# Pooled attention with a SoLU layer: v as 128 consecutive pooled rows per pair of heads, first loads in another order, all orders planned anew

## The chip, the cores and the metric

One core of one Trainium2 chip runs the whole kernel. Times are device microseconds (us). Lower is better. Three runs of the kernel before gave 516.31, 513.35 and 512.03 us; their median, 513.35 us, is the time that the changed kernel is compared with.

## The reference

Eight batches, eight heads, 576 rows of 64 numbers. k and v are pooled over eight rows each, so that every head has 72 pooled rows:

```python
k_p = k.reshape(B, H, 72, 8, D).mean(axis=3)
v_p = v.reshape(B, H, 72, 8, D).mean(axis=3)
scores = q @ k_p^T / sqrt(D)
attn = softmax(scores)
x = (attn @ v_p), heads side by side     # 4608 tokens x 512
h = x @ w_in                             # w_in 512 x 1024, float64
solu = h * softmax(h)
ln = (solu - mean) / sqrt(var + 1e-6) * g_ln
out = ln @ w_out                         # w_out 1024 x 512, float64
```

The weights arrive as float64; everything else is float32.

## The kernel before, in words

The 4608 tokens are 36 tiles of 128. Every float32 operand of a large product is split into a high and a low half in float16, and a product is taken in three passes (high x high, high x low, low x high). Per tile: `q_hi`, `q_lo` split q, a DMA transpose (`q_T`, L805) turns it, TensorE makes `scores` (L842), VectorE and ScalarE make the softmax (`s_max` L852, `s_sub` L855, `s_exp` L862, `e_sum` L866, `e_rec` L872 and L876, `e_mul` L881), ScalarE and GpSimd split it (`e_hi`, `e_lo`), a DMA transpose turns it (`e_T`, L917), TensorE multiplies it by v (`av`, L928), `x_hi` and `x_lo` (L936, L940) split the result, and `mm1` (L957) multiplies it by w_in in three parts of 8 matmuls. `h_max`, `h_nb`, `h_exp`, `z_mul`, `z_cen`, `z_hi`, `z_lo` make the layer (L967 to L1019), `z_T` (L1027) turns it, `mm2` (L1066) multiplies it by w_out in three parts of 8 matmuls, `o_evac` (L1074) scales it out of PSUM, and a store follows.

PSUM holds one buffer of scores, one of `av`, two of `mm1`'s result and one of `mm2`'s result. So `mm1` of a tile waits for `z_mul` of the tile two before it, and `mm2` of a tile waits for `o_evac` of the tile before it.

Before the first tile, the weights are prepared. Each weight is loaded in four quarters of 1 MiB (`w_load`, L563). A quarter of w_in goes through `w_exp` (ScalarE, L574), `w_shift` (VectorE, L578), `w_bnd` (TensorE, L590), `w_tail` (VectorE, L597), `w_sgn` (ScalarE, L615) and `w_mul` (GpSimd, L618). Only when all four quarters have passed `w_bnd` can the largest value be found (`w_rmax`, `w_par`, `w_all`) and the scale be set (`wi_scale`, last instruction L653). After it `w_hi` (L720), `w_res` (L741) and `w_lo` (L757) write the two halves of w_in that `mm1` reads.

k and v of a batch come in three loads each (`load_kv`): parts 0 and 1 of 512 KB, part 2 of 128 KB. k's lines (L336, L340) put 128 consecutive pooled rows of all heads on 128 partitions. v's lines differ: part 0 (L343) puts rows 0 to 63 of the four even heads on partitions 0 to 63, part 1 rows 0 to 63 of the four odd heads on partitions 64 to 127, and part 2 (L348) puts the last 8 rows of every head on 64 partitions. GpSimd adds the eight rows up in three levels (`pool_kv`, L380); for v, the first level of parts 0 and 1 waits for both loads. `a_max`, `a_par`, `a_all`, `a_scale` find a batch's scale. `v_hi` (L507, ScalarE) and `v_lo` (L513, VectorE) write the split v into `vb`, 64 partitions at a time, `v_rep`, `r_hi`, `r_lo` copy the left-over rows, and `r_put` (GpSimd, L543, two instructions of 256 columns) places them, masked by `rmask`.

All DMAs are issued by SyncE's queue (SP) in one order. The order of every operation is written out by hand in `ORDER`: for each operation name a tuple of positions, and all operations are emitted in order of position. An engine takes its own operations in that order and never overtakes. `load_g` (L673) loads g_ln, 1024 single numbers. In the order before, SP's queue begins (k, v parts in brackets, q halves, w_in quarters w0 to w3, w_out quarters A to D):

```
k[0] k[2] w0 k[1] q0 q1 g w1 w2 v[0] v[1] w3 v[2] B A q_T(1) D C ...
```

VectorE's list between the arrival of w1 and the scale of w_in is, before: `w_shift` w1, `w_tail` w1, `q_lo`(1), k's `a_max`, `w_shift` w2, `q_lo`(3), `w_tail` w2, k's `a_all` and `a_scale`, `k_lo`, `w_shift` w3, `s_scale`, `s_max`, `s_sub`, `w_rmax`, `w_tail` w3, `e_sum`, `e_rec`, `e_mul`, `w_all`, v's `a_max`, `wi_scale`.

Of the kernel before, what the change touches and what calls it, by code (L numbers as in the profile page):

```python
# [1446 lines left out]
```

## Time and profile before

| | us |
|---|---|
| median of three runs | 513.35 |
| profiled execution, whole | 516.21 |
| its span, first to last instruction | 514.4 |
| TensorE (PE) busy in the span | 468.7 (91%) |
| VectorE (DVE) | 366.3 (71%) |
| ScalarE (ACT) | 331.5 (64%) |
| GpSimd (POOL) | 327.6 (64%) |

Times in the rows are of the span. PE is the matmul side of TensorE, PEld its weight loads, SPq SyncE's queue. An arrow in brackets behind a row says how long the engine was idle before it and what it then waited for. The profiled execution ran 1.8 us longer than its span and 2.9 us longer than the median of the three runs.

### The profile page before, as it was taken

Reading aid. Unit: us, or ns where it says so; the run is one execution under the profiler, and the core shown is the slowest. Engines: PE = TensorE matmul, PEld = TensorE weight load, DVE = VectorE, ACT = ScalarE, POOL = GpSimd, SP = SyncE. Lnnn points to the kernel's source line nnn. Section 1 sums busy time; section 2 is a strip of 40 time slices with the busy share of each in tenths; the row PEclk is TensorE's granted clock in tenths of the full one; section 3 lists DMA queues with packets and bytes.
Section 4 is the critical chain, followed back from the end, with each engine's and each line's share of the span. In section 5 each row is a group of like instructions: output and inputs, shape, how many; then the busy total and the mean of one; then the engine's idle time right before and its main releaser. Section 6 shows DMA issues by size and latency. Waiting matters only on the chain.

```text
span 514.4 us, 9219 instructions
## 1 busy us (share of the span) xinstructions
PE 468.7 (91%) x3236; PEld 247.9 (48%) x3236; DVE 366.3 (71%) x777; ACT 331.5 (64%) x515; POOL 327.6 (64%) x554
## 2 busy tenths in 40 slices
PE   0227999999999999999999999999999989999996
PEld 0114545554465555555555555554554445454442
DVE  3669998989778775879588888776568678755230
ACT  2529987877766675667486775667647655667541
POOL 5463778887982767567967678656938335645331
PEclk9999999999999999999999999999999999999999
DMA  7998938696997978898999489978599655655433
GB/s 253 257 276 242 247 65 190 121 213 150 209 204 123 198 166 170 141 223 206 198 173 196 99 138 267 177 158 187 134 184 188 125 114 109 123 106 104 89 90 93
DMA packets 189501, 86.26 MB, mean 168 GB/s; under 512 B 165904, under 2 KB 174096, under 8 KB 188944
## 3 DMA queue, kind: packets, MB, share of 16 engines
q1 hardware_dynamic: 189456, 85.69, 79.2%
q8 instruction: 25, 0.41, 0.3%
q14 instruction: 20, 0.16, 0.1%
HBM read 36.70 MB, written 9.44 MB: 90 GB/s over the span
## 4 chain that ended last, share of the span: by engine, by line
PE 74%; DMA 7%; DVE 5%; ACT 5%; issue 3%; POOL 3%; SPq 2%; POOLq 0%; ACTq 0%; DVEq 0%
PE hp L957 33%; PE op L1066 29%; PE xp L928 6%; DMA wir<-in_moe_w_in_dram 4%; PE sc L842 4%; DMA qT<-q 2%; DMA eT<-e 1%; SPq L563 1%; POOL z L1019 1%; PE res_wi L741 1%; DVE u_wi L578 1%; DVE z L999 1%; PE kTp L475 1%; DVE m L967 1%; SPq L673 1%
## 5 line engine op out<-in xcount | busy, mean ns | idle before, releaser
L1066 PE MATMUL op<-wo,zT 128*128 128x512 f16 x864 | 198.1, 379 | 1.8 <-ACT osb L1074 1.7
L957 PE MATMUL hp<-wi,xT 128*128 128x512 f16 x864 | 196.2, 379 | 0.5 <-ACT xT L936 0.5
L957 PEld LDWEIGHTS <-xT 128*128 128x128 f16 x864 | 83.1, 98 | 97.3 <-ACT xT L936 1.0
L1066 PEld LDWEIGHTS <-zT 128*128 128x128 f16 x864 | 82.3, 98 | 93.4 <-issue 2.5
L1019 POOL TENSOR_TENSOR z<-z,z 128x512 f16<-128x512 f32 x71 | 83.0, 1176 | 59.7 <-ACT z L1013 59.5
L967 DVE TENSOR_REDUCE m<-hp 128x1 f32<-128x1024 f32 x36 | 43.9, 1219 | 30.9 <-PE hp L957 30.7
L906 POOL TENSOR_TENSOR e<-e,e 128x512 f16<-128x512 f32 x36 | 42.3, 1175 | 31.5 <-ACT e L897 31.5
L380 POOL TENSOR_TENSOR vr<-vr 128x512 f32<-128x512 f32 (+3 forms) x48 | 41.6, 875 | 19.3 <-DMA vr<-in_v_dram 18.9
L999 DVE SCALAR_TENSOR_TENSOR z<-hp,rs,z 128x1024 f32<-128x1024 f32 x36 | 46.1, 1280 | 10.8 <-ACT z L978 9.8
L1008 ACT ACTIVATE z<-z,sz 128x1024 f32<-128x1024 f32 x36 | 41.2, 1144 | 17.8 <-DVE z L999 17.7
L978 ACT ACTIVATE z<-hp,nb,Hb 128x1024 f32<-128x1024 f32 x32 | 38.4, 1199 | 19.4 <-DVE nb L970 15.9
L380 POOL TENSOR_TENSOR kr<-kr 128x512 f32<-128x512 f32 (+3 forms) x48 | 42.2, 886 | 12.5 <-DMA kr<-in_k_dram 11.6
L1074 ACT ACTIVATE osb<-op,f 128x512 f32<-128x512 f32 x36 | 24.5, 680 | 24.6 <-issue 16.1
L852 DVE TENSOR_REDUCE mx<-sc 128x8 f32<-128x576 f32 x36 | 27.1, 752 | 17.2 <-PE sc L842 17.2
L928 PE MATMUL xp<-eT,vb 128*128 128x128 f16 (+1 forms) x640 | 38.2, 214 | 0.8 <-DMA eT<-e 0.8
L1013 ACT ACTIVATE z<-z 128x1024 f16<-128x1024 f32 x36 | 37.8, 1051 | 1.2 <-DMA zT<-z 0.6
L928 PEld LDWEIGHTS <-vb 128*128 128x128 f16 x640 | 34.8, 98 | 7.2 <-DMA eT<-e 1.3
L1032 ACT ACTIVATE junk<-z 128x1024 f16<-128x1024 f32 x36 | 37.7, 1047 | 0.1
L897 ACT ACTIVATE e<-e 128x512 f16<-128x512 f32 x36 | 22.4, 623 | 20.3 <-DVE e L881 14.0
L866 DVE TENSOR_REDUCE sc<-sc 128x8 f32<-128x576 f32 x36 | 27.4, 761 | 9.7 <-ACT sc L862 9.6
L936 ACT ACTIVATE xT<-xp 128x512 f16<-128x512 f32 x36 | 21.3, 591 | 19.9 <-PE xp L928 19.7
L940 DVE SCALAR_TENSOR_TENSOR xT<-xp,xT 128x512 f16<-128x512 f32 x36 | 24.5, 682 | 10.9 <-ACT xT L936 10.9
(226 smaller groups left out, 626.3 us busy)
## 6 DMA issues: line engine op xcount, KB each, us to landing
kr<-in_k_dram SPq DMA_DIRECT2D x16, 512.0 KB, 4.6
qr<-in_q_dram SPq DMA_DIRECT2D x16, 512.0 KB, 5.2
vr<-in_v_dram SPq DMA_DIRECT2D x16, 512.0 KB, 9.7
out_dram<-osb SPq DMA_DIRECT2D x32, 256.0 KB, 3.3
wor<-in_moe_w_out_dram SPq DMA_DIRECT2D x4, 1024.0 KB, 8.4
wo<-in_moe_w_in_dram SPq DMA_DIRECT2D x2, 1024.0 KB
wir<-in_moe_w_in_dram SPq DMA_DIRECT2D x2, 1024.0 KB, 12.1
zT<-z SPq DMA_TRANSPOSE x72, 3.3
```

Source lines behind the costliest of these rows:

```text
L380: nc.gpsimd.tensor_tensor(out=dst, in0=src[:, :, :n], in1=src[:, :, n : 2 * n], op=ALU.add)
L906: nc.gpsimd.tensor_tensor(out=e_main(i, 1), in0=e_src(i)[:, :, :64], in1=e_main(i, 0), op=ALU.subtract)
L928: nc.tensor.matmul(xp[:, c, lo:hi], lhsT=vb[b % 2][:, vt, c].rearrange("p j d -> p (j d)"), rhs=eT[:, n, lo:hi], start=(j == 0), stop=(j = ...
L957: nc.tensor.matmul(hp[:, f], lhsT=xT[:, xt, c], rhs=wi[:, wt, c, f * 512 : (f + 1) * 512], start=(c == 0 and xt == 0 and wt == 0), stop=(c ...
L967: nc.vector.tensor_reduce(out=small(i, "m"), in_=tl[i]["hp"], axis=AX.XY, op=ALU.max)
L978: nc.scalar.activation(z, t["hp"], AF.Exp, bias=t["nb"], scale=hsc(i, 0), accum_out=small(i, "se"))
L999: nc.vector.scalar_tensor_tensor(out=t["z"], in0=t["hp"], scalar=t["rs"], in1=t["z"], op0=ALU.mult, op1=ALU.mult, accum_out=small(i, "sz"),)
L1008: nc.scalar.activation(t["zf"], t["zf"], AF.Identity, bias=t["sz"], scale=-float(DFF))
L1013: nc.scalar.activation(t["z16"][:, 0], t["zf"], AF.Copy)
L1019: eng.tensor_tensor(out=t["z16"][:, 1, fs], in0=t["zf"][:, fs], in1=t["z16"][:, 0, fs], op=ALU.subtract)
L1032: nc.scalar.activation(junk, t["zf"], AF.Square, scale=DFF**-0.5, accum_out=small(i, "V"))
L1066: nc.tensor.matmul(op_, lhsT=zT[:, zt, c], rhs=wo[:, wt, c], start=(c == 0 and zt == 0 and wt == 0), stop=(c == CO - 1 and zt == 1),)
```

## The change

Pooled rows are now counted per pair of heads: a pair has 144 consecutive pooled rows. The first 128 of them lie on 128 partitions, one column block per pair, and the last 16 (all of the odd head) are the left-over rows. Parts 0 and 1 of a v load are two pairs each, 128 partitions by 4 KB; part 2 is the 16 rows of the four pairs, on 64 partitions as before. On the 128 partitions, rows 0 to 71 belong to the even head and rows 72 to 127 to the odd head, so `v_hi` and `v_lo` write all 128 partitions of a head's columns with a scale that is zero outside its rows. A new VectorE operation, `v_msk`, multiplies the batch's scale by a fixed mask of two columns; `v_hi` and `v_lo` wait for it. `r_put` places the left-over rows for the odd heads alone, two instructions of 128 columns. The softmax side (`e_main`, `e_rest`, `e_src`) is cut the same way: four runs of 128 and four of 16 in place of eight of 64 and eight of 8. `v`'s first pooling level of a part waits for that part alone.

The planner's list of first loads is `"01kq2v3gABCD"` in place of `"0kq12v3gABCD"`, and `ORDER` is written anew. SP's queue now begins:

```
k[0] g w0 k[1] q0 k[2] q1 w1 v[0] w2 w3 v[2] v[1] A B q_T(1) C D ...
```

VectorE's list between the arrival of w1 and the scale of w_in is now: `w_shift` w1, `q_lo`(0), `w_tail` w1, `q_lo`(3), k's first `a_scale`, `w_shift` w2, `q_lo`(1), `w_tail` w2, `w_shift` w3, two `a_scale`, `k_lo`, `w_rmax`, `s_max`, `s_sub`, `s_scale`, `e_sum`, `e_rec`, `e_mul`, `w_tail` w3, `w_all`, `wi_scale`, and then v's `a_max`. ScalarE's list there is: `w_exp` w1, `q_hi`(0), `q_hi`(3), `w_sgn` w1, `w_exp` w2, `q_hi`(1), `w_exp` w3, `w_sgn` w2, `k_hi`, `q_Tc`, `w_exp` A, `s_exp`, `w_sgn` B, `w_exp` B, `e_hi`, `w_sgn` w3, `w_dg`, `w_hi`. At the end of the list, TensorE's parts stand as `mm1`(34) part 2, `mm2`(33) parts 1 and 2, `mm2`(32), `mm2`(35), `mm2`(34); before, `mm2`(33) stood ahead of `mm1`(34) part 2.

```diff
 ORDER = {
...
-    "load_g": (6,),
...
-    "load_q": (4, 5, 116, 132, 377, 415, 618, 707, 906, 955, 1171, 1217, 1379, 1425, 1656, 1755),
...
-    "w_load": (2, 7, 8, 20, 30, 28, 57, 55),
...
+    "load_g": (4,),
+    "load_kv": (0, 10, 16, 46, 66, 64, 158, 170, 163, 230, 237, 232, 282, 321, 316, 330, 407,
...
+    "load_q": (12, 24, 152, 154, 426, 438, 640, 703, 901, 933, 1159, 1210, 1410, 1427, 1665, 1762),
...
+    "v_msk": (116, 346, 587, 840, 1100, 1254, 1510, 1861),
...
+    "w_load": (5, 34, 48, 54, 78, 87, 120, 121),
...
+    vmask = const.tile([P, 2], F32, name="vmask")
...
+    for j, cs in enumerate((slice(0, SP), slice(SP, P))):
+        nc.vector.tensor_reduce(out=vmask[:, j : j + 1], in_=ident[:, cs], axis=AX.X, op=ALU.max)
...
+        rows = v[b].rearrange("h (r j) d -> (h r) (j d)", j=POOL).rearrange(
+            "(c r) x -> r c x", c=CI
+        )
         if part < 2:
-            eng.dma_start(
-                t[64 * part : 64 * part + 64, :CI],
-                v[b].rearrange("(c e) (r j) d -> e r c (j d)", e=2, j=POOL)[part, :64],
-            )
-        else:
-            eng.dma_start(
-                t[:64, CI], v[b, :, SA:].rearrange("h (r j) d -> h r (j d)", j=POOL)
-            )
+            eng.dma_start(t[:, c0:c1], rows[:P, c0:c1])
+        else:
+            eng.dma_start(t[:64, CI], rows[P:])
...
+    def v_msk(b):
+        st = grp["v", b]
+        st["sm"] = sm.tile([P, 2], F32, tag="smv", name=f"smv{b}")
+        nc.vector.tensor_scalar(
+            out=st["sm"], in0=vmask, scalar1=st["s"], scalar2=None, op0=ALU.mult
+        )
+
     def v_hi(b, e):
-        r_ = slice(64 * e, 64 * e + 64)
         nc.scalar.activation(
-            vb[b % 2][r_, 0, :, e], vp[b % 2][r_, :CI], AF.Copy, scale=grp["v", b]["s"][r_]
+            vb[b % 2][:, 0, :, e], vp[b % 2][:, :CI], AF.Copy,
+            scale=grp["v", b]["sm"][:, e : e + 1],
         )
...
-                out=vb[b % 2][:, 2, 2 * j : 2 * j + 2].rearrange("p c e d -> p (c e) d"),
-                in0=bat[b]["vr16"][:, j].unsqueeze(1).to_broadcast([P, 4, D]),
-                in1=rmask.unsqueeze(2).to_broadcast([P, 4, D]), op=ALU.mult,
+                out=vb[b % 2][:, 2, 2 * j : 2 * j + 2, 1],
+                in0=bat[b]["vr16"][:, j].unsqueeze(1).to_broadcast([P, 2, D]),
+                in1=rmask.unsqueeze(2).to_broadcast([P, 2, D]), op=ALU.mult,
...
-        return e16[i % 2][:, t * SA : t * SA + SA].rearrange("p (h r) -> p h r", h=H)
+        return e16[i % 2][:, t * SA : t * SA + SA].rearrange("p (c r) -> p c r", c=CI)
...
-            if nm == "v" and part < 2:
-                rk = [("rp", "vr", b, e) for e in range(2)]
...
-    for n, c in enumerate("0kq12v3gABCD"):
+    for n, c in enumerate("01kq2v3gABCD"):
```

## Rows read from the trace of the kernel before

**Rows 1.** Busy time of each engine in stretches of the span, all engines in one line: the stretch and its length in us, then busy us and instructions of PE, PEld, DVE, ACT and POOL, the granted clock, the mean busy share of the DMA engines and GB/s.

```profile
0.00:43.00 43.00, 7.35 (x67) 5.39 (x68) 24.99 (x47) 17.05 (x21) 23.81 (x33) 1.00 0.98 277
43.00:61.00 18.00, 17.84 (x123) 10.33 (x124) 17.45 (x36) 17.80 (x24) 8.56 (x8) 1.00 0.87 213
61.00:80.00 19.00, 17.91 (x115) 9.31 (x112) 16.34 (x39) 16.55 (x27) 14.91 (x22) 1.00 0.49 101
80.00:360.00 280.00, 279.87 (x1980) 148.78 (x1980) 220.92 (x479) 191.85 (x308) 203.27 (x349) 1.00 0.88 178
360.00:480.00 120.00, 117.11 (x822) 61.22 (x821) 78.79 (x164) 76.04 (x121) 68.00 (x124) 1.00 0.69 132
480.00:514.00 34.00, 28.60 (x140) 12.89 (x137) 7.83 (x16) 12.20 (x17) 9.09 (x22) 1.00 0.36 85
```

**Rows 2.** The timeline of ScalarE and VectorE at the arrival of w_in's quarters: start, duration, instruction, and the idle time ahead of it. The first two are `w_exp` of quarter 1 and of quarter 3, the third is `w_shift` of quarter 3.

```profile
17.49 1.13 ACT L574 ACTIVATE u_wi<-wo 128x1024 f32<-128x1024 f32 x1 [0.40 <-DMA wo<-in_moe_w_in_dram]
...
32.26 1.12 ACT L574 ACTIVATE u_wi<-wir 128x1024 f32<-128x1024 f32 x1 [3.22 <-DMA wir<-in_moe_w_in_dram]
...
33.41 3.90 DVE L578 TENSOR_SCALAR u_wi<-u_wi 128x1024 int32<-128x1024 int32 x1 [3.52 <-ACT u_wi L574]
```

**Rows 3.** The timeline from the scale of w_in to the first tile's `mm1`: the last instructions of `wi_scale`, then `x_lo` of tile 0 and the first matmuls of `mm1`.

```profile
43.41 0.26 DVE L653 TENSOR_SCALAR pw<-pwi 128x1 f32<-128x1 f32 x3
...
59.55 0.68 DVE L940 SCALAR_TENSOR_TENSOR xT<-xp,xT 128x512 f16<-128x512 f32 x1
...
60.97 5.34 PE L957 MATMUL hp<-wi,xT 128*128 128x512 f16 x24
```

**Rows 4.** The same table of stretches as rows 1, for three stretches of the first 35 us; the last column is what the DMA engines moved, in GB/s.

```profile
9.00:17.00 8.00, 1.14 (x10) 0.79 (x10) 5.73 (x9) 2.99 (x4) 5.79 (x5) 1.00 1.07 362
19.00:27.00 8.00, 1.34 (x11) 0.95 (x12) 5.30 (x9) 5.31 (x7) 2.50 (x1) 1.00 1.07 169
29.00:35.00 6.00, 1.33 (x24) 1.22 (x23) 2.41 (x2) 1.15 (x2) 5.01 (x5) 1.00 1.20 361
```

**Rows 5.** SP's queue in the timeline: when it issued a load and how long the issue took it: w0, g, w1, and both large parts of v in one row.

```profile
1.95 0.58 SPq L563 DMA_DIRECT2D wo<-in_moe_w_in_dram  x1
...
4.19 3.34 SPq L673 DMA_DIRECT2D g_sb<-in_moe_g_ln_dram  x1
7.57 3.68 SPq L563 DMA_DIRECT2D wo<-in_moe_w_in_dram  x1
...
11.77 1.50 SPq L343 DMA_DIRECT2D vr<-in_v_dram  x2
```

**Rows 6.** The page's list of DMA issues: count, KB each, and the median us from issue to landing.

```profile
kr<-in_k_dram SPq DMA_DIRECT2D x16, 512.0 KB, 4.6
...
vr<-in_v_dram SPq DMA_DIRECT2D x16, 512.0 KB, 9.7
```

**Rows 7.** The timeline of the steps that stand ahead of the scale of w_in: `w_sgn` of quarter 2, `k_hi`, `k_lo`, `scores`, `s_max`, `s_sub`, `s_exp`, `w_tail` of quarter 3, `e_sum`, `e_mul`, `w_all`, and `a_max` of v.

```profile
25.29 1.14 ACT L615 ACTIVATE sg_wi<-wir 128x1024 f16<-128x1024 f32 x1
28.29 0.74 ACT L483 ACTIVATE kT<-kTp,sk 128x576 f16<-128x576 f32 x1 [1.50 <-PE kTp L475]
29.07 0.82 DVE L487 SCALAR_TENSOR_TENSOR kT<-kTp,sk,kT 128x576 f16<-128x576 f32 x1 [1.27 <-ACT kT L483]
...
29.94 1.12 PE L842 MATMUL sc<-kT,qT 128*128 128x72 f16 x16 [1.68 <-DVE kT L487]
...
38.13 0.77 DVE L855 TENSOR_TENSOR sc<-sc,mx 128x576 f32<-128x576 f32 x1
38.99 0.71 ACT L862 ACTIVATE sc<-sc,ct('b', 0)_291 128x576 f32<-128x576 f32 x1 [5.61 <-DVE sc L855]
39.14 1.22 DVE L597 SCALAR_TENSOR_TENSOR wir<-wir,u_wi 128x1024 int32<-128x1024 int32 x1
...
41.51 0.76 DVE L881 TENSOR_TENSOR e<-sc,r 128x576 f32<-128x576 f32 x1
42.18 0.28 DVE L630 TENSOR_REDUCE gm_wi<-g_wi 128x1 f32<-128x128 f32 x1
42.38 0.48 DVE L391 TENSOR_REDUCE amx_v<-vp 128x1 f32<-128x320 f32 x1
```

**Rows 8.** Groups of instructions by line and shape over the whole span (count, busy us, mean ns of one): `r_put` and `v_hi`; then ScalarE's copy of k on 128 partitions.

```profile
L543 POOL TENSOR_TENSOR vb<-vr,rmask 128x256 f16<-128x256 f16 x16 | 9.8, 637 | 3.2 <-DVE vr L536 2.5 <-ACT q L793 0.7
L507 ACT ACTIVATE vb<-vp,sv 64x256 f16<-64x256 f32 x16 | 8.0, 501 | 3.3 <-DVE sv L464 3.2
...
L468 ACT ACTIVATE kp<-kp 128x320 f32<-128x320 f32 x8 | 3.7, 463 | 0.8 <-POOL kp L380 0.8
```

**Rows 9.** What TensorE waited for after 60 us, summed: us in total, times, longest.

```profile
PE op L1066 <- ACT osb L1074: 1.7, 2, 0.9
PE sc L842 <- DMA qT<-q: 1.6, 1, 1.6
...
PE xp L928 <- DMA eT<-e: 0.8, 1, 0.8
```

**Rows 10.** Groups of instructions from the page: `h_max`, `z_mul` and `h_exp`, with the mean ns of one behind the busy time.

```profile
L967 DVE TENSOR_REDUCE m<-hp 128x1 f32<-128x1024 f32 x36 | 43.9, 1219 | 30.9 <-PE hp L957 30.7
...
L999 DVE SCALAR_TENSOR_TENSOR z<-hp,rs,z 128x1024 f32<-128x1024 f32 x36 | 46.1, 1280 | 10.8 <-ACT z L978 9.8
...
L978 ACT ACTIVATE z<-hp,nb,Hb 128x1024 f32<-128x1024 f32 x32 | 38.4, 1199 | 19.4 <-DVE nb L970 15.9
```

More of the change, by code (lines that the diff above doesn't have):

```diff
@@ L153 @@
-    "v_hi": (133, 125, 363, 349, 643, 578, 879, 837, 1170, 1174, 1285, 1297, 1500, 1507, 1833,
-        1826),
-    "v_lo": (151, 147, 371, 376, 655, 665, 894, 892, 1176, 1183, 1289, 1299, 1509, 1513, 1842,
-        1838),
-    "v_rep": (119, 342, 582, 832, 1161, 1280, 1493, 1837),
-    "w_all.wi": (98,),
-    "w_all.wo": (192,),
-    "w_bnd.wi": (22, 45, 75, 80),
-    "w_bnd.wo": (139, 165, 167, 170),
-    "w_dg.wi": (120,),
-    "w_dg.wo": (227, 205),
-    "w_exp.wi": (13, 38, 48, 71),
-    "w_exp.wo": (90, 103, 129, 140),
@@ new lines @@
+    "e_mul": (86, 151, 197, 258, 345, 390, 417, 484, 526, 615, 680, 656, 808, 841, 866, 911, 970,
+        1042, 1105, 1163, 1212, 1276, 1333, 1370, 1477, 1417, 1552, 1642, 1603, 1695, 1750, 1818,
+        1871, 1903, 1986, 1952),
+    "e_rec": (84, 85, 140, 141, 187, 193, 255, 256, 339, 341, 388, 389, 413, 415, 461, 472, 524,
[4 rows of a table added]
+    "e_sum": (83, 136, 186, 249, 334, 387, 412, 459, 523, 610, 676, 646, 796, 819, 863, 906, 966,
+        1026, 1102, 1131, 1197, 1256, 1330, 1357, 1463, 1404, 1526, 1624, 1596, 1690, 1729, 1810,
+        1852, 1891, 1983, 1946),
@@ new lines @@
+    "g_all": (27,),
+    "g_max": (14,),
+    "g_par": (15,),
+    "h_bat": (133, 400, 580, 896, 1178, 1265, 1660, 1867),
+    "h_exp": (215, 296, 350, 398, 452, 513, 554, 706, 649, 746, 772, 912, 928, 949, 1007, 1048,
+        1114, 1216, 1239, 1304, 1363, 1429, 1485, 1547, 1572, 1629, 1698, 1792, 1752, 1835, 1905,
+        1926, 1987, 2018, 2061, 2046),
+    "h_max": (209, 272, 318, 362, 447, 493, 536, 704, 647, 734, 768, 875, 922, 946, 1004, 1021,
+        1112, 1202, 1233, 1295, 1355, 1378, 1476, 1528, 1555, 1612, 1686, 1765, 1723, 1831, 1873,
+        1912, 1977, 2001, 2058, 2038),
@@ new lines @@
+    "h_mix": (402, 903, 1346, 1886),
+    "h_nb": (210, 273, 319, 382, 448, 504, 537, 705, 648, 735, 769, 878, 923, 947, 1005, 1022,
+        1113, 1203, 1236, 1296, 1359, 1395, 1479, 1540, 1556, 1613, 1687, 1766, 1730, 1832, 1875,
+        1913, 1979, 2002, 2059, 2039),
+    "k_T": (58, 280, 571, 695, 1050, 1300, 1437, 1761),
+    "k_dup": (33, 278, 501, 681, 963, 1171, 1408, 1634),
+    "k_hi": (61, 299, 572, 740, 1062, 1301, 1440, 1780),
+    "k_lo": (62, 300, 586, 741, 1063, 1302, 1441, 1786),
@@ new lines @@
+    "r_hi": (137, 356, 591, 850, 1176, 1289, 1518, 1856),
+    "r_lo": (139, 360, 594, 859, 1180, 1291, 1522, 1857),
+    "r_put": (159, 361, 641, 861, 1181, 1293, 1681, 1869),
+    "s_exp": (82, 134, 185, 246, 333, 385, 399, 458, 518, 609, 672, 645, 784, 814, 862, 905, 964,
+        1025, 1101, 1126, 1196, 1255, 1329, 1356, 1461, 1403, 1521, 1623, 1595, 1674, 1728, 1804,
+        1851, 1890, 1975, 1943),
+    "s_max": (74, 105, 169, 212, 311, 365, 396, 446, 503, 589, 670, 624, 766, 812, 845, 877, 953,
+        1009, 1076, 1124, 1174, 1235, 1327, 1350, 1459, 1394, 1506, 1620, 1569, 1671, 1708, 1802,
+        1843, 1884, 1958, 1938),
@@ new lines @@
+    "v_hi": (130, 129, 367, 354, 593, 592, 849, 883, 1127, 1141, 1285, 1263, 1520, 1519, 1862,
+        1863),
+    "v_lo": (149, 148, 375, 376, 607, 596, 880, 893, 1133, 1169, 1299, 1274, 1565, 1563, 1874,
+        1870),
+    "v_msk": (116, 346, 587, 840, 1100, 1254, 1510, 1861),
+    "v_rep": (118, 355, 590, 843, 1175, 1288, 1517, 1846),
+    "w_all.wi": (95,),
+    "w_all.wo": (194,),
+    "w_bnd.wi": (9, 37, 69, 70),
+    "w_bnd.wo": (142, 143, 165, 166),
+    "w_dg.wi": (97,),
+    "w_dg.wo": (228, 202),
@@ new lines @@
+    "w_exp.wi": (6, 35, 49, 55),
+    "w_exp.wo": (79, 89, 122, 127),
+    "w_hi.wi": (145, 108, 126, 175),
+    "w_hi.wo": (205, 201, 303, 309),
+    "w_lo.wi": (176, 135, 174, 191),
+    "w_lo.wo": (252, 240),
+    "w_load": (5, 34, 48, 54, 78, 87, 120, 121),
+    "w_lod.wo": (304, 347),
+    "w_mul.wi": (23, 63, 76, 107),
+    "w_mul.wo": (161, 132, 224, 295),
+    "w_par.wi": (93,),
+    "w_par.wo": (192,),
+    "w_res.wi": (146, 109, 144, 189),
+    "w_res.wo": (229, 220),
+    "w_rmax.wi": (71,),
@@ new lines @@
+    "w_rmax.wo": (180,),
+    "w_sgn.wi": (22, 44, 57, 92),
+    "w_sgn.wo": (160, 88, 196, 294),
+    "w_shift.wi": (7, 36, 50, 56),
+    "w_shift.wo": (110, 111, 150, 147),
+    "w_tail.wi": (8, 41, 53, 94),
+    "w_tail.wo": (131, 128, 162, 204),
+    "wi_scale": (96,),
+    "wo_scale": (200,),
+    "x_hi": (179, 219, 269, 308, 378, 450, 495, 627, 603, 685, 742, 767, 868, 917, 940, 989,
+        1019, 1152, 1204, 1270, 1309, 1336, 1407, 1462, 1537, 1571, 1647, 1724, 1683, 1779, 1816,
+        1883, 1950, 1962, 2041, 2005),
```

245 lines of the change are left out of this document (94 added, 151 removed), and 96 rows, old and new, of the table ORDER.

## The prediction

> **What bounds the kernel now.** I read the table of stretches first [rows 1]. From 80 to 360 us TensorE is busy for 279.87 of 280 us, and from 360 to 480 for 117.11 of 120. No engine can make that part shorter, since the change takes no matmul away. What is left is the head and the end: before 43 us TensorE is busy for 7.35 us, so 35.65 are empty, and 43 to 80 and 480 to 514 hold 1.25 and 5.40 more. A gain of some size can only come out of the 35.65.
>
> Next, what the head waits for. ScalarE idles until each quarter of w_in lands: quarter 1 at 17.49, quarter 3 only at 32.26, after 3.22 us with nothing to do [rows 2]. The scale of w_in needs all four quarters, and it is done at 43.41 + 0.26 = 43.67; the first `mm1` starts at 60.97 [rows 3]. The head is therefore a chain: last quarter landed, 11.41 us to the scale, 17.30 us to `mm1`.
>
> Why does quarter 3 land so late? The rates of the transfers say it [rows 4]: 362 GB/s from 9 to 17 us, 361 from 29 to 35, but 169 from 19 to 27. In that stretch the two large parts of v are under way, issued at 11.77 behind w2 and ahead of w3 [rows 5]. Over the whole run a v load of 512 KB takes 9.7 us to land and a k load of the same size 4.6 [rows 6]. The v loads fill 64 partitions, the k loads 128.
>
> **The change, part by part.** *First loads.* Up to w1 both orders carry the same bytes (k, q, w0, w1: 4.125 MiB), so I keep 17.49 as w1's landing and correct it below for g. Before, w2, v[0], v[1] and w3 (3 MiB) came behind it; now it is v[0], w2 and w3 (2.5 MiB = 2.62 MB), and v no longer on half of the partitions. At 361 GB/s that takes 7.26 us: w3 lands at 24.75. The other end, with v as slow as now: 0.524 MB at 169 GB/s and 2.10 MB at 361 are 8.9 us, 26.4. I take the first, since k's parts already have the shape that v's now get.
>
> g moves from behind q1 to the second place, ahead of w0. Its issue held SP's queue for 3.34 us [rows 5]. In front of w0 it could move w0's issue from 1.95 to about 4.6, 2.65 us; but k[0] is being moved meanwhile, and before the change SP was held from 4.19 to 11.25 by g and w1 in a row, ahead of w1, which no longer stands behind g. Bounds 0 and 2.65; I take 0.5, near the lower end for that reason. So w3 at 25.25, 7.0 us earlier. The queue's other moves (v[2], v[1], A, B and the first q transpose come right behind) are each earlier than now, as the bytes ahead are no more.
>
> *From w3 to the scale.* With w3 this early, the k side is no longer done first: VectorE's new list puts `k_lo` and the softmax of tile 0 behind `w_shift` w3, and `w_tail` w3 and the scale behind that softmax. Link by link: `w_exp` 1.12 [rows 2], then `w_sgn` w2 1.14, `k_hi` 0.74, `k_lo` 0.82, `scores` 1.12, `s_max` about 0.75, `s_sub` 0.77, `s_exp` 0.71, `e_sum` about 0.75 (both like `e_mul`), `e_rec` about 0.4, `e_mul` 0.76, `w_tail` 1.22, `w_all` 0.28 [rows 7], and 0.9 for the scale: 11.5, with some 0.05 at each of ten hand-overs (`k_hi` to `k_lo`, 0.04, [rows 7]) and 0.2 for `q_Tc` 12.2. The same stretch was 11.41, so 0.8 of the 7.0 is given back: scale at 37.5, 6.2 earlier.
>
> *From the scale to `mm1`.* From 43.67 to the start of `x_lo` at 59.55 VectorE works without a pause to speak of [rows 1, 3]. Its list there is the old one plus v's `a_max` (0.48, [rows 7]) and `v_msk` (0.26 for three such small instructions, [rows 3]; 0.15 with its hand-over). 0.6 more is given back: `mm1` starts 5.6 us earlier, at 55.4. From there TensorE is full, as now.
>
> *`v_hi`, `v_lo`.* 128 partitions in place of 64 with the same columns. ScalarE's copy of 320 columns on 128 partitions takes 463 ns, `v_hi` with 256 on 64 takes 501 [rows 8]: partitions cost nothing. *`v_msk`* stands ahead of both once a batch; from the second batch on TensorE's full list covers it. If that cover went, 8 x 0.15 = 1.2 us. *`r_put`* halves its columns, 0.3 us less of GpSimd each of 16 times [rows 8], hidden, as GpSimd idles a third of the span. *The softmax side* has the same elements in longer runs; nothing. *Masks and memsets* fall before 4 us, when everything waits for loads; nothing.
>
> *Steady part.* The v loads of batches 1 to 7 also land faster, and the waits of TensorE for transposes, 1.6 and 0.8 [rows 9], may shrink. Bounds 0 and 2.4; I take 0.8 gained. *End.* TensorE now runs `mm2`(33) straight into `mm2`(32), 35 and 34: three hand-overs of its one PSUM buffer instead of two, each like the 0.9 in rows 9: 0.9 lost.
>
> **Sum.** 7.0 - 0.8 - 0.6 + 0.8 - 0.9 = 5.5 us. Against the profiled execution: span 514.4 to 508.9, whole 516.21 to 510.7. That execution ran 2.9 us over the median of 513.35; the median becomes 507.8.
>
> **The rivals.**
>
> *A, the forecast: 507.8.* Its own range 505.5 to 510, from g (0 to 2.65) and the steady part. 56%.
>
> *B, VectorE gives more back: 511.* `w_shift` w3 took 3.90 us here though ScalarE had long delivered, [rows 2], in a stretch in which GpSimd was busy for 5.01 of 6 us [rows 4]. Were the head's chain hit by one such stretch more, 3.2 us of the 5.5 are gone. For it: GpSimd's new list has pooling and `w_mul` all along. Against: `w_tail` w3 now comes when the pooling of v should be over. 15%.
>
> *C, v gets no faster, only the order counts: 510.* w3 then lands at 26.4 + 0.5, 5.4 earlier; less 0.8, 0.6 and 0.9, and with nothing gained in the steady part, 3.1: 510.2. Against it: k's 4.6 us beside v's 9.7. 9%. [...]
>
> *D, more: 504.8.* g costs nothing (0.5), and all of the waits for transposes go (1.6 more) with the end's third hand-over hidden (0.9): 8.5. 11%.
>
> *E, slower: 519.* The new list starts a tile's `mm1` sooner behind that of two tiles before: at its closest (tiles 14 and 16) one tile's `mm1` and one `av` and `scores` lie between, about 6.6 us, where the closest before was 8.4. In that time `h_max`, `h_exp` and `z_mul` must run, 3.7 us of work [rows 10], and VectorE has other work queued between them. If the new plan is this tight everywhere, TensorE stalls. It decides when the 36 tiles lose over 10.6 us together, 0.3 each, enough to turn the 5.5 into 5.1 lost; at 0.3 to 0.35 each it is 518.6 to 520.4. For it: TensorE has no room. Against: the old list, nearly as tight, loses 0.13 in 280 us [rows 1]. 9%.
>
> **How the numbers follow.** A measurement of this kernel can tell about 1% from no change, 5.1 us; the bound is 508.2. Of A somewhat more than half lies under it (0.33), and D (0.11), with a little of B and C: 0.47 faster. E is 0.09 slower. The rest, 0.44, is within 1%. The predicted time is A's 507.8. The range goes from 504.5 to 512: it takes in B, C and nearly all of A and D and leaves out E and D's lower end.
>
> **What would show it.** Right: v loads land in about 5 us; the rate stays over 330 GB/s until w3; `w_exp` of quarter 3 starts at 24.5 to 27; the scale ends near 37.5 and `mm1` starts near 55.4; TensorE is as full from there as now. Wrong at the first step, if `w_exp` of quarter 3 starts after 28; at the second, if it is early but the scale is after 40; at the third, if `mm1` is early but TensorE's empty time after 61 us grows by more than 2.

## The result, and the profile after

The changed kernel takes 520.43 us, the median of four runs (518.95 to 522.54). The kernel before took 514.75, the median of four runs on the same chip: the three of 513.35 and one more of 516.15. The ratio is 1.0118, with a 95% interval from 1.0081 to 1.0155: slower by about 1.2%, where 507.8, a gain, was forecast, and outside the range of 504.5 to 512. The profiled execution took 521.71 us, with a span of 520.0 against 514.4 before.

The table of stretches of the changed kernel, with the columns of [rows 1]. The last stretch runs 2 us past the end of the span; up to 520 us its clock is 1.00.

```profile
0.00:43.00 43.00, 11.11 (x89) 7.88 (x90) 30.06 (x58) 22.33 (x27) 26.71 (x35) 1.00 1.01 327
43.00:61.00 18.00, 16.99 (x127) 8.59 (x127) 17.59 (x37) 14.98 (x20) 13.58 (x11) 1.00 0.29 71
61.00:80.00 19.00, 16.28 (x96) 8.19 (x93) 15.06 (x30) 15.73 (x28) 15.03 (x22) 0.91 0.61 130
...
80.00:360.00 280.00, 273.80 (x1941) 144.82 (x1941) 227.28 (x476) 185.98 (x300) 196.01 (x338) 1.00 0.81 172
360.00:480.00 120.00, 120.00 (x832) 62.75 (x830) 81.21 (x173) 75.62 (x121) 65.85 (x120) 1.00 0.68 139
480.00:522.00 42.00, 33.15 (x164) 15.07 (x161) 8.36 (x18) 16.12 (x22) 14.42 (x31) 0.98 0.38 88
```

Set against [rows 1], the empty time of TensorE reads as follows. Before 43 us it fell from 35.65 to 31.89, 3.8 gained. From 43 to 80 us it grew from 1.25 to 3.73, and from 80 to 360 from 0.13 to 6.20: 8.6 lost. From 360 to 480 all of the 2.89 went, and the end, up to the end of the span, grew from 5.8 to 6.9. That makes 2.9 us more of empty time, and the busy time grew by 2.65 (471.32 against 468.67), together the 5.6 of the spans. One cell says why the engine was busy for longer with the same products: the granted clock, 0.91 between 61 and 80 us. It accounts for 1.7 of the 2.65; the rows do not explain the other 0.9.

What TensorE waited for after 60 us (us in total, times, longest), to be held against [rows 9]:

```profile
PE op L1076 <- ACT osb L1084: 3.4, 4, 0.9
PE res_wo L751 <- DVE z L1009: 2.7, 1, 2.7
PE sc L852 <- DVE e L891: 2.5, 3, 1.4
```

The waits for transposes of q are gone. In their place stand waits for VectorE, which [rows 9] do not have, and the hand-overs of the output's PSUM buffer have doubled in all: at the end there are three (2.5 us) for two (1.7), and the fourth lies between 80 and 160 us.

The head, in the timeline: `w_shift` of quarter 2, `w_exp` of quarter 3, `w_tail` of quarter 2, `w_shift` of quarter 3, `k_hi`, the last instructions of the scale, and the first product. They answer to [rows 2, 3].

```profile
22.48 2.54 DVE L588 TENSOR_SCALAR u_wi<-u_wi 128x1024 int32<-128x1024 int32 x1
...
23.98 1.15 ACT L584 ACTIVATE u_wi<-wir 128x1024 f32<-128x1024 f32 x1 [1.20 <-DMA wir<-in_moe_w_in_dram]
...
26.09 2.28 DVE L607 SCALAR_TENSOR_TENSOR wir<-wir,u_wi 128x1024 int32<-128x1024 int32 x1
...
28.29 1.21 DVE L588 TENSOR_SCALAR u_wi<-u_wi 128x1024 int32<-128x1024 int32 x1
...
29.85 0.74 ACT L486 ACTIVATE kT<-kTp,sk 128x576 f16<-128x576 f32 x1 [3.70 <-DVE sk L467]
...
39.27 0.26 DVE L663 TENSOR_SCALAR pw<-pwi 128x1 f32<-128x1 f32 x3
...
56.00 1.89 PE L967 MATMUL hp<-wi,xT 128*128 128x512 f16 x8
```

The transfers did what was forecast. In the page's list of DMA issues v now lands like k, in 4.7 us where [rows 6] had 9.7:

```profile
vr<-in_v_dram SPq DMA_DIRECT2D x16, 512.0 KB, 4.7
```

**The costliest place.** The longest single wait, in the timeline: GpSimd's `e_lo` and VectorE's `w_tail` of w_out's last quarter, then `h_max` and `z_mul` of the first tile, then TensorE's `w_res`.

```profile
62.09 1.41 POOL L916 TENSOR_TENSOR e<-e,e 128x512 f16<-128x512 f32 x1 [2.76 <-ACT e L907]
62.40 2.18 DVE L607 SCALAR_TENSOR_TENSOR wor<-wor,u_wo 128x1024 int32<-128x1024 int32 x1
...
64.51 1.21 DVE L977 TENSOR_REDUCE m<-hp 128x1 f32<-128x1024 f32 x1
...
67.46 1.28 DVE L1009 SCALAR_TENSOR_TENSOR z<-hp,rs,z 128x1024 f32<-128x1024 f32 x1 [0.19 <-ACT z L988]
...
69.01 1.69 PE L751 MATMUL res_wo<-wor,dg_wo 128*128 128x512 f32 x2 [2.72 <-DVE z L1009]
```

`w_res` wants the PSUM buffer that holds the first tile's products until `z_mul` has read them. `z_mul` stands behind `h_max`, `h_max` in VectorE's list behind a `w_tail` that took 2.18 us beside GpSimd (1.21 in the kernel before). TensorE stands for 2.72 us. What follows shows in TensorE's own table of single microseconds (busy us, granted clock, DMA share, GB/s):

```profile
68.00:69.00 1.00, 0.00 (x0) 1.00 0.77 223
69.00:70.00 1.00, 0.99 (x2) 0.70 0.71 272
70.00:71.00 1.00, 1.00 (x3) 0.50 0.00 0
71.00:72.00 1.00, 1.00 (x3) 0.50 0.00 0
72.00:73.00 1.00, 1.00 (x3) 0.59 0.00 0
73.00:74.00 1.00, 1.00 (x6) 1.00 0.00 0
```

The engine comes back at a granted clock of 0.50 instead of 1.00 and stays there for some 3.4 us. One minus the clock, summed over these rows, is another 1.71 us lost, without a single empty slot. A table of busy shares alone hides it. In the kernel before the same place had a wait of 1.1 us and a clock of 1.00 throughout. Its `w_tail` of w_out's last quarter, and the `w_res` that waited:

```profile
65.50 1.21 DVE L597 SCALAR_TENSOR_TENSOR wor<-wor,u_wo 128x1024 int32<-128x1024 int32 x1
...
71.05 1.14 PE L741 MATMUL res_wo<-wor,dg_wo 128*128 128x512 f32 x2 [1.09 <-ACT xT L936]
```

### The profile page after: what moved, and what is told of

Same layout as the page of the kernel before. It is cut to its first block, busy times and chain, and to the rows that moved or that the text cites. A ratio compares the mean times of both kernels' runs of the same rounds, so it can differ in the third digit from the quotient of the medians.

```text
span 520.0 us, 9226 instructions
## 1 busy us (share of the span) xinstructions
PE 471.3 (91%) x3236; PEld 247.3 (48%) x3236; DVE 379.6 (73%) x787; ACT 330.8 (64%) x515; POOL 331.6 (64%) x554
## 4 chain that ended last, share of the span: by engine, by line
PE 64%; DVE 22%; ACT 5%; issue 4%; DMA 3%; SPq 1%; POOL 1%; ACTq 0%; DVEq 0%; POOLq 0%
PE op L1076 28%; PE hp L967 26%; PE xp L938 4%; DVE q L807 3%; PE sc L852 3%; DMA wo<-in_moe_w_in_dram 2%; DVE z L1009 2%; DVE m L977 2%; DVE sc L876 2%; DVE e L891 1%; DVE wor L607 1%; DVE sc L865 1%; DVE mx L862 1%; DMA zT<-z 1%; ACT z L988 1%
## 5 line engine op out<-in xcount | busy, mean ns | idle before, releaser
L916 POOL TENSOR_TENSOR e<-e,e 128x512 f16<-128x512 f32 x36 | 43.4, 1204 | 57.0 <-ACT e L907 57.0
L383 POOL TENSOR_TENSOR kr<-kr 128x512 f32<-128x512 f32 (+3 forms) x48 | 44.3, 933 | 13.9 <-DMA kr<-in_k_dram 13.4
L383 POOL TENSOR_TENSOR vr<-vr 128x512 f32<-128x512 f32 (+3 forms) x48 | 43.4, 913 | 9.1 <-DMA vr<-in_v_dram 5.4
L852 PE MATMUL sc<-kT,qT 128*128 128x72 f16 (+1 forms) x640 | 27.2, 201 | 9.5 <-DVE e L891 6.6
L852 PEld LDWEIGHTS <-qT 128*128 128x128 f16 (+1 forms) x640 | 24.7, 104 | 17.3 <-issue 11.7
```

The lines of the kernel that those rows point to most:

```text
L383: nc.gpsimd.tensor_tensor(out=dst, in0=src[:, :, :n], in1=src[:, :, n : 2 * n], op=ALU.add)
L852: nc.tensor.matmul(o, lhsT=t["qT"][:, h, lo:hi], rhs=kT[:, x, h * SP : (h + 1) * SP], start=(x == 0), stop=(x == 1),)
L916: nc.gpsimd.tensor_tensor(out=e_main(i, 1), in0=e_src(i)[:, :, :P], in1=e_main(i, 0), op=ALU.subtract)
```

## The experiments

Theory 1: the new order puts VectorE's instructions with two inputs in SBUF (`q_lo`, with a mean of 0.87 us before and 1.10 in the changed kernel), and fast small ones (`v_msk`, with a median of 0.23 us and 0.83 at the longest), beside GpSimd's work; each is held up, VectorE works in order, and TensorE stops. Theory 2: the new order's own hand-overs of PSUM. Theory 3: the new layout costs it. All edits are against the changed kernel, but for the one of the order alone, and each ratio is to the kernel before, run on the same chip. The runs were made on more than one chip, so where two of them are set against each other, their ratios say more than their times.

**The layout alone.** The order table is that of the kernel before, with the mask behind v's third scale:

```diff
-    "load_g": (4,),
+    "load_g": (6,),
...
-    "w_load": (5, 34, 48, 54, 78, 87, 120, 121),
+    "w_load": (2, 7, 8, 20, 30, 28, 57, 55),
...
```

> The changed kernel's layout of v (128 consecutive rows, mask, r_put of half the size, whole e tiles) with the order of the kernel before, every instruction in its old place and the new mask right behind the third scale of v. Theory 1 (the new order puts VectorE's two-input and fast instructions beside GpSimd's, where they hold each other up) and theory 2 (the new order's own hand-overs of PSUM) both say: no loss, 510 to 515 us, and q_lo's mean back near 0.87 us. Theory 3 (the layout costs it: the mask, the halves of v on 128 partitions, e in another shape): 518 us or more, near the changed kernel's 520.

Measured: 514.96 us, ratio 1.0011 (0.9977 to 1.0046). Theory 3 falls as the main cause: the 5.5 us are the order's. But the layout brings nothing in the median either, though its first product starts at 55.05. Its profile shows two places where that is given back. From 160 to 360 us TensorE is empty for 2.13 us; in three profiles of the kernel before it was 0.00 to 0.76, and 0.9 of it is a wait of `av` that stands in every profile of the layout with the old steady order and in none of those three. The other place is shown here: GpSimd's pooling, the mask `v_msk`, v's first half, the copy of a tile's sums, and the last product's groups.

```profile
135.21 2.36 POOL L383 TENSOR_TENSOR kr<-kr 64x256 f32<-64x256 f32 x3
...
135.65 1.53 DVE L511 TENSOR_SCALAR smv<-vmask,sv 128x2 f32<-128x2 f32 x1
...
137.28 0.51 ACT L516 ACTIVATE vb<-vp,smv 128x256 f16<-128x256 f32 x1 [3.50 <-DVE smv L511]
...
137.69 0.67 ACT L1084 ACTIVATE osb<-op,f 128x512 f32<-128x512 f32 x1
...
138.41 3.15 PE L1076 MATMUL op<-wo,zT 128*128 128x512 f16 x8 [1.60 <-ACT osb L1084]
```

An instruction that writes two numbers per partition took 1.53 us, and ScalarE's list stood still behind it. The table of stretches has the clock (third column from the right):

```profile
138.00:140.00 2.00, 1.59 (x5) 0.60 (x5) 1.57 (x3) 1.94 (x4) 0.90 (x3) 0.72 1.10 186
140.00:142.00 2.00, 2.00 (x11) 1.09 (x10) 1.33 (x4) 1.51 (x2) 1.34 (x3) 0.50 1.10 270
142.00:144.00 2.00, 2.00 (x19) 1.29 (x18) 0.47 (x1) 1.10 (x2) 1.81 (x5) 0.93 0.58 111
```

1.60 us of standing and 2 x (0.28 + 0.50 + 0.07) = 1.70 at the lower clock.

**The new head before the old steady order, and the reverse.**

```diff
-    "mm2": (363, 371, 372, 383, 420, 421, 442, 483, 497, 582, 583, 584, 540, 541, 543, 601, 604,
+    "mm2": (314, 350, 358, 377, 388, 399, 432, 446, 487, 558, 565, 576, 523, 536, 545, 588, ...
```

> The changed kernel's layout and its order up to the third product of the first tile (209 instructions), then the order of the kernel before. If the head's gain of 3.5 us holds and the loss is the order after it (theories 1 and 2): 508 to 512 us, first product still near 56 us, TensorE's loss after 61 us no larger than before's. If the head's gain is given back whatever comes after it, because something behind the first tile (keys and queries of the second batch) sets the start of the stretch that is full: 513 to 516. If the layout costs it (theory 3): 518 or more.

> The changed kernel's layout, the order of the kernel before up to the third product of the first tile (205 instructions) and the changed order from there. The run with the new head and the old steady order took 521.8 us, so the head's order alone carries the loss. If that is the whole of it: 513 to 516 here, like the old order throughout (515.0). If the new steady order loses as well (q_lo beside GpSimd's work at 141 and 149 us): 518 to 521, with TensorE's loss between 95 and 155 us 4 us larger than in the old order.

Measured: new head 521.81 (1.0139; 1.0065 to 1.0213), old head with the new steady order 515.75 (1.0027; 1.0005 to 1.0048). My first expectation had it the wrong way round: I looked for the loss in the steady order, and the time moved with the first 209 instructions. In the run with the new head TensorE's wait of `w_res` at 67 us was 3.2 us, and its clock between 61 and 80 us 0.82. The new steady order costs 0.8 us behind the old head (515.75 against 514.96) and takes 1.4 off behind the new one (520.43 against 521.81); the intervals of the ratios overlap in both pairs. That is a balance and not an absence of loss. With the old head the new steady order has 3.99 us empty between 80 and 160, as the changed kernel has 5.09; the new head before the old steady order has 1.48:

```profile
80.00:160.00 80.00, 76.01 (x553) 40.12 (x554) 70.31 (x139) 51.89 (x84) 57.13 (x94) 1.00 0.76 160
```

Most of the loss there is the steady order's, and it wins much of it back from 360 to 480, where it has no empty time and the old one 2.2 to 2.9. The loss at 61 to 80 us is the head's. Each of the two runs also has a seam between two orders, and what that costs by itself no run shows.

**Less pooling on GpSimd, in both orders.** The kernel leaves out two of the three adding levels of every batch but the first; it is a probe and no kernel to use.

```diff
+        if lvl < 2 and b > 0:
+            return
         if lvl < 2:
             dst = src[:, :, :n]
```

> The changed kernel with the first two of the three adding levels of k's and v's pooling left out for every batch but the first: these batches pool 2 of 8 rows, which leaves GpSimd about a quarter of that work, and VectorE's instructions and their order as they are. Theory 1 (VectorE held up beside GpSimd): q_lo's mean falls from 1.10 us to 0.85 or less, the loss on TensorE between 61 and 155 us shrinks by 5 us or more, and the time is 512 to 515. Theory 2 (hand-overs of the new order): 518 to 521, TensorE's loss between 61 and 155 us as it is.

> The same pooling left out in the layout of the changed kernel with the order of the kernel before. Theory 1: the two orders come together, within 3 us of the changed order with the same work left out, and below 513. Theory 2: the old order stays 5 to 8 us ahead, near 510 to 514.

Measured: new order 514.16 (0.9992), old order 510.80 (0.9933). The stretch from 80 to 160 us, new order and then old:

```profile
80.00:160.00 80.00, 78.92 (x580) 41.99 (x578) 66.94 (x147) 55.26 (x89) 42.34 (x80) 1.00 0.78 169
```

```profile
80.00:160.00 80.00, 79.96 (x565) 42.50 (x562) 66.45 (x145) 56.78 (x94) 43.58 (x86) 1.00 0.80 168
```

TensorE's empty time there falls from 5.09 (80 less the 74.91 that the same stretch of the changed kernel has) to 1.08 us, the mean of batch 2's `q_lo` from 2443 to 886 ns (of all `q_lo` from 1.10 to 0.87 us; 0.85 was said), and the two orders come within 3.4 us of each other (3 was said). Theory 1's time came out, its 5 us less of loss were 4.0. The wait at 66 us is not touched (2.7 us again); in the changed kernel its `w_tail` stood beside `e_lo`, not beside pooling. The run takes away GpSimd's lateness together with the holding up, so it does not separate the two.

**One instruction moved.**

```diff
-    "w_tail.wo": (131, 128, 162, 204),
+    "w_tail.wo": (131, 128, 162, 216),
```

> The changed kernel with one VectorE instruction moved: the tail of the last quarter of w_out, which took 2.18 us beside GpSimd at 62.4 us (1.21 us undisturbed), goes behind the first tile's z_mul. Theory 1 (a blocked instruction, in order ahead of h_max and z_mul, keeps the PSUM buffer that w_res.wo0 wants): TensorE's wait of 2.7 us at 66.3 us falls to 1 us or less, the stretch at the lower clock behind it (69.3 to 72.7 us, 1.7 us lost) goes with it, and the time is 515.5 to 518. Theory 2 (the new order gives that hand-over too little cover whatever VectorE does): the wait stays above 2 us and the time at 519 to 521.

The positions in between move up by one. Measured: 518.30 us (1.0078; 1.0049 to 1.0108), 2.1 less than the changed kernel, with nine runs between 517.93 and 518.96, just outside the expectation. `z_mul` and `w_res` again:

```profile
66.22 1.28 DVE L1009 SCALAR_TENSOR_TENSOR z<-hp,rs,z 128x1024 f32<-128x1024 f32 x1 [0.46 <-ACT z L988]
...
67.77 1.14 PE L751 MATMUL res_wo<-wor,dg_wo 128*128 128x512 f32 x2 [1.65 <-DVE z L1009]
```

The wait falls by 1.07 us, and the clock behind it stays at 1.00. Against the two runs of the changed kernel whose mean clock was 1.000 (518.95, 519.15) that is 0.75 us, against the two others (521.71, 522.54) 3.8. But 1.65 us of the wait stay, where I had said 1 or less: so much of it belongs to the order, as theory 2 has it. No VectorE instruction of the chain is held up in this run (`h_max` 1.22 us, `z_mul` 1.28).

**The mask on another engine, in the old order.**

```diff
-        nc.vector.tensor_scalar(
-            out=st["sm"], in0=vmask, scalar1=st["s"], scalar2=None, op0=ALU.mult
-        )
+        nc.scalar.activation(st["sm"], vmask, AF.Copy, scale=st["s"])
```

> The old order with the new layout again, but the mask of v (128x2, one instruction per batch) is made by ScalarE right ahead of the first half of v, and no longer by VectorE. In the run with the mask on VectorE one of them took 1.53 us beside pooling at 135.7 us of the span (0.23 us where GpSimd is quiet), v's first half waited 3.5 us for it, the copy of a tile's sums behind that on ScalarE came late, TensorE stood 1.6 us and then ran at the lower clock until 143 us: 3.2 us lost. If blocked VectorE instructions are what gives the head's gain back: that loss is gone, TensorE's clock is 1.00 between 80 and 160 us, and the time is 511 to 513. If it is any lateness of the pooled rows of v (the chain behind them, not the mask): 514 to 516, with a like stall near 137 us.

Measured: 513.03 us (0.9981; 0.9958 to 1.0003), 1.9 less than with the mask on VectorE. The intervals of the two ratios overlap, so the times alone do not show the gain; the rows show the stall gone. The mask takes 0.29 us there, and the copy behind it starts at 136.06 instead of 137.69:

```profile
135.26 0.29 ACT L511 ACTIVATE smv<-vmask,sv 128x2 f32<-128x2 f32 x1 [1.65 <-DVE sv L467]
...
136.06 0.67 ACT L1084 ACTIVATE osb<-op,f 128x512 f32<-128x512 f32 x1
```

From 80 to 160 us TensorE is busy for 79.82 us at a clock of 1.00, against 78.36 at 0.98.

**The first loads' sequence alone.** As the last, with the first 17 loads in the changed kernel's sequence:

```diff
-    "load_g": (6,),
+    "load_g": (1,),
...
-    "w_load": (2, 7, 8, 20, 30, 28, 57, 55),
+    "w_load": (2, 7, 9, 14, 28, 30, 55, 57),
```

> The run with the mask on ScalarE in the old order (513.0 us), with the first 17 loads in the changed kernel's sequence and all else in the old order: what the other order of the first loads does alone. If the landing of w_in's last quarter sets the scale (the prediction's first step): its decoding on ScalarE starts 3 us or more earlier than 28.4 us, the scale is earlier by as much as VectorE allows, and the time is 510 to 512. If VectorE's chain of held-up instructions sets it (scale at 38.0 us with w_in's last quarter last, 39.5 us in the changed kernel with it early): 512.5 to 515, the first product no earlier than 55 us.

Measured: 516.63 us (1.0030; 1.0004 to 1.0056), 3.6 more, or 2.5 by the ratios, and outside both expectations. `k_hi` and `w_exp` of quarter 3 without the edit and with it:

```profile
27.22 0.74 ACT L486 ACTIVATE kT<-kTp,sk 128x576 f16<-128x576 f32 x1 [4.32 <-DVE sk L467]
27.86 1.13 ACT L584 ACTIVATE u_wi<-wir 128x1024 f32<-128x1024 f32 x1
```

```profile
30.68 0.74 ACT L486 ACTIVATE kT<-kTp,sk 128x576 f16<-128x576 f32 x1 [7.17 <-DVE sk L467]
31.32 1.14 ACT L584 ACTIVATE u_wi<-wir 128x1024 f32<-128x1024 f32 x1
```

Neither row of `w_exp` waits for a DMA: with v on 128 partitions the landing of quarter 3 is off the path of the old order, and `k_hi` ahead of it on ScalarE is on it. The new sequence moves k's last part behind q, the old GpSimd list wants that part first, and k comes 3.5 us later. The run is therefore no clean test of the sequence in its own order; it shows that loading w_in earlier buys nothing unless k is ready as well.

**The order alone.** The kernel before with the changed order (v's second load ahead of the first pooling, where it was behind):

```diff
-    "w_load": (2, 7, 8, 20, 30, 28, 57, 55),
+    "w_load": (5, 34, 49, 55, 78, 87, 119, 120),
```

> The kernel before, v on 64 partitions at a time and no mask, with the new order of instructions (v's second load ahead of the first pooling where that order had it behind, in four batches). If the new order costs its 5 us on either layout: 518.5 to 523, with a long wait of w_res.wo for PSUM near 66 us and TensorE's clock down behind it. If order and layout only lose together (the order was planned for the layout): 513 to 516.

Measured: 531.74 us (1.0337; 1.0288 to 1.0386), outside both expectations. The order needs the layout that it was planned with; on the old one waits of 4.5 us for `z_scale` and 3.3 for a transpose of z come to those already seen.

**How typical was the one profile of before?** Nothing is changed in three of these four runs; the last repeats the mask on ScalarE.

> The kernel before, unchanged, profiled again: is its one profile typical? If its head is as late in every execution: first product near 61 us and any lower time comes from after it. If that profile had a late head: a run near 513 us starts its first product 2 to 3 us earlier, with w_in's last quarter landing earlier than 32.3 us.

> The kernel before once more, with the same two readings: first product near 61 us whatever the time, or earlier by what the run is faster than 516.2 us.

> The changed kernel, unchanged, profiled again. First product within 0.5 us of 56.0, the wait of w_res.wo at 66 us again over 2 us; if the clock falls behind it the time is near 522, if it stays up near 519.

> The old order with the mask on ScalarE, profiled again (513.0 median, but 510.9 in the profile). If the head's gain holds in each execution: first product near 55 us again, and any time over 511 is lost after it, by a stall with the clock down or by waits for transposes. If the head scatters: first product later by what the run is slower.

Measured: 510.88, 515.25, 522.05 and 515.38 us, one run each. The changed kernel repeats itself: first product at 56.34, the wait of `w_res` 2.7 us, the mean clock over the run 0.997 in both profiles. With the mask on ScalarE the first product starts at 55.85, and the stall at 137 us does not come back (the longest wait for the copy of a tile's sums is 0.9 us); the time goes later: TensorE waits 1.9 us for a transpose of q and up to 1.5 for `x_hi`, at a mean clock of 0.997 over the run, where the first profile had 2.0, 0.6 and 1.000. `w_exp` of quarter 3 and the first product in the two new profiles of before, which answer to 32.26 and 60.97 in [rows 2, 3]:

```profile
26.87 1.16 ACT L574 ACTIVATE u_wi<-wir 128x1024 f32<-128x1024 f32 x1 [1.31 <-DMA wir<-in_moe_w_in_dram]
...
55.18 5.34 PE L957 MATMUL hp<-wi,xT 128*128 128x512 f16 x24
```

```profile
30.77 1.12 ACT L574 ACTIVATE u_wi<-wir 128x1024 f32<-128x1024 f32 x1 [2.99 <-DMA wir<-in_moe_w_in_dram]
...
59.35 5.34 PE L957 MATMUL hp<-wi,xT 128*128 128x512 f16 x24
```

The head of the kernel before scatters by 5.8 us, and its time with it (516.21, 515.25, 510.88). With v on 128 partitions the first product started between 54.87 and 56.99 in eight profiles, and at 58.33 in the one with the new load sequence in the old order. So the profile of before that I had was its latest head of three.

**The version that beats both.** New layout, mask on ScalarE, old order up to the first product of tile 24 (1535 instructions), new order behind it, which has no waits for transposes of q:

```diff
-    "k_hi": (61, 299, 572, 740, 1062, 1301, 1440, 1780),
+    "k_hi": (68, 290, 559, 702, 1065, 1301, 1434, 1780),
...
```

> New layout, mask of v on ScalarE, old order up to the first product of tile 24 and the new order from there. In the old order TensorE lost 3.3 us between 350 and 395 us of its own work done (e7: scores wait 2.0 us for a transpose of q), in the new one 0.9; the new order's end costs about 1 us more in hand-overs of the output's PSUM buffer. If the stretches simply add: 511 to 512.5, below e7's 513.0 and clearly below before (ratio under 0.998). If the seam of the two orders opens a stall of its own, or the old order's stall on the transpose is only scatter: 513 or more.

Measured: 510.79 us, ten runs from 509.23 to 512.74, ratio 0.9925 (0.9896 to 0.9954), against 515.14 for the kernel before on that chip. The longest wait of its TensorE after 60 us:

```profile
PE hp L967 <- ACT xT L946: 1.3, 1, 1.3
```

None is for a transpose of q, and from 360 to 480 us TensorE is busy for all of the 120. The stretches added as expected; the median is 0.2 us under the range that was said.

## Why the prediction was wrong

**The landing of quarter 3: right.** `w_exp` started at 23.98, forecast 25.25. v lands in 4.7 us, and the rate stayed high (353 GB/s from 9 to 17 us, 379 from 17 to 24). g's issue in the second place took 0.45 us, the value I chose was 0.5, where behind q1 it had held the queue for 3.34 [rows 5]. Rival C, in which v stays at the 9.7 us of [rows 6], falls with it.

**From there to the scale: mis-sized.** 39.53 less 23.98 is 15.55 us, and the sum said 12.2. The sum had `k_hi` wait for ScalarE alone, 2.3 us behind `w_exp`; it came 5.87 us behind, because it waited 3.70 us for k's scale, which stands in VectorE's list behind `w_shift` of quarter 3. Nearly all of the 3.4 us lie there. Four of VectorE's instructions ahead of that scale took longer than alone: `w_shift` of quarter 2 took 2.54 us and not 0.69, a `q_lo` 1.22 and not 0.74, `w_tail` of quarter 2 2.28 and not 1.22, `w_shift` of quarter 3 1.21 and not 0.69. This is the mechanism of rival B, and near its price of 3.2, at several places for its one. The scale came 2.0 us later than forecast, still 4.1 before [rows 3].

**From the scale to `mm1`: slightly better.** 16.47 us, where 17.9 were forecast; the first product at 56.00 for 55.4.

**"From there TensorE is full, as now": this step failed.** I had named its sign, an empty time after 61 us that grows by more than 2 with `mm1` early. It grew from 9.9 to 15.8 us, and 1.7 more went to the clock. In the terms of the sum: from the first product to the end of the span the kernel before took 453.4 us and the changed one 464.0, 10.6 more, where the steady part and the end were to cost 0.1 together. That turns the 5.0 us by which the first product came earlier into a loss of 5.6. I costed the head and took the rest from the row of the old order, but the order was new from the first instruction to the last. Nothing in [rows 1] says how full another order keeps TensorE. The forecast's own argument against rival E, that the old list loses 0.13 us in 280, was a statement on the old list.

**Rival E named the right time (518.6 to 520.4) for the wrong reason.** It wanted every tile a little late, `mm1` waiting for `z_mul`; after 60 us no `mm1` of the changed kernel waits for anything in the list of waits. The runs show a few places in the first third: the wait at 66 us with its clock, and the stretch from 80 to 160 us with 5.09 of the 6.20 us that are empty up to 360.

**`v_msk` "at nothing, covered by TensorE's full list": wrong.** TensorE is full, but the mask's neighbours on VectorE and ScalarE are not free to wait. I priced it at 0.15 us from rows of small instructions that stood alone. In the old order one of eight took 1.53, and the stall behind it went when the mask left VectorE. In the changed kernel itself the longest of the eight took 0.83, and what it cost there no run shows.

**"The median becomes 507.8": wrong by itself.** I took a gain off the median that was measured against one execution with a late head. Where the head was early, the kernel before reached 510.88 without any change. Against the middle of the three heads (59.35) the changed kernel's first product gains 3.4 us and not 5.0, against the earliest it loses 0.8.

**The steady part and the end.** From 360 to 480 us all of the 2.89 us of empty time went, 2.4 of them waits for transposes (forecast 0.8 gained, upper bound 2.4). The hand-overs at the end rose from 1.7 to 2.5 us, as forecast (0.9). Together these two gained 2.1 us where the sum had 0.1 lost; they are not where it failed.

**What holds VectorE up.** In the changed kernel a `q_lo` of 0.74 us took 3.86, while GpSimd's went by one after the other, and `k_lo`, and with it the scores, waited behind it:

```profile
141.34 3.86 DVE L807 SCALAR_TENSOR_TENSOR q<-qr,sq('b', 2)_1358,q 128x512 f16<-128x512 f32 x1
...
141.59 0.45 POOL L383 TENSOR_TENSOR kr<-kr 64x128 f32<-64x128 f32 x1
...
142.01 1.15 POOL L916 TENSOR_TENSOR e<-e,e 128x512 f16<-128x512 f32 x1
...
143.38 2.40 POOL L383 TENSOR_TENSOR kr<-kr 128x512 f32<-128x512 f32 x2
...
145.38 0.80 DVE L490 SCALAR_TENSOR_TENSOR kT<-kTp,sk,kT 128x576 f16<-128x576 f32 x1
```

`h_max`, which reads its tile from PSUM, is not touched: it has the same mean in both kernels, here and in [rows 10] (1219 ns there).

```profile
L977 DVE TENSOR_REDUCE m<-hp 128x1 f32<-128x1024 f32 x36 | 43.9, 1218 | 40.1 <-PE hp L967 40.0
```

Four kinds of instruction that took longer read no PSUM: `q_lo` (3.86 us here, 0.74 alone), `w_tail` (2.28, 1.22), `w_shift` (2.54, 0.69) and the mask (1.53, 0.23). Why these are held up beside GpSimd and `h_max` is not, no run shows. Over the span VectorE was busy for 13.3 us more than before (379.6 against 366.3) with eight small instructions added.

What stays open: how much of the 5.09 us between 80 and 160 is this holding up and how much the closer order of hand-overs. Less pooling took 4.0 of it away, but eases both.

## What to carry to other kernels

When a change brings a new order of all instructions, the fullness of the bottleneck engine is a term of the sum like any other, and the old row gives no price for it; ask of the first stretch above all which in-order list a held-up instruction can stop. Price an added VectorE instruction by its row beside busy GpSimd, not alone (the mask took 1.53 us and 0.23), and put a small one that others wait for on an engine that the rows do not show held up beside GpSimd, as ScalarE here (0.29 beside pooling). Take two or three profiles of the kernel before ahead of costing its head: here the landing of the last early load differed by 5.4 us between executions of one program, and by 3.9 between two on the same chip.

## What was not expected of the hardware

A stop of TensorE of 2.72 us was followed by some 3.4 us at a granted clock of 0.50, and so it cost 4.4. A stop of 1.60 us (at 137 us of the run with the layout alone, behind the short products of `scores` and `v_rep`) was followed by the lower clock as well (0.50 from 140 to 142 us); one of 1.65 (with the one instruction moved) was not (1.00 from 66 to 78 us). The length of the stop alone does not decide it: with the mask on ScalarE the same wait for a transpose of q was 2.0 us long in one profile, with a mean clock of 1.000 over the run, and 1.9 in the other, with 0.997; where that run lost its clock is not shown. The changed kernel's four runs lie in two groups: 518.95 and 519.15 at a mean clock of 1.000, 521.71 and 522.54 at 0.997 and 0.995. Of the two profiles that there are, the one of 521.71 us shows the drop, and the one of 522.05 has the same wait of 2.7 us and the same mean clock of 0.997; that the others had none is read from their mean clock alone.

The `q_lo` that was held up beside GpSimd did not simply come next: while it stood, from 141.34 to 145.20 us, five GpSimd instructions began, and it took 3.1 us longer than alone.
